# A new order of transfers and works in the opening of a RetNet and gelu kernel

The kernel computes a recurrent attention block and a feed-forward block behind it. The change touches the first 30 microseconds or so: which transfers go first, how TensorE is kept busy before its first data arrive, which of two operands is transposed first, and where the conversion of the weights stands among VectorE's other works.

## The chip, the cores and the metric

The kernel runs on one core of a Trainium2 chip. Its engines are TensorE (PE; PEld is its loading of weights), VectorE (DVE), ScalarE (ACT), GpSimd (POOL) and SyncE (SP), which here only issues transfers. The metric is the device time of one execution in microseconds (us); the figure quoted is the median of three.

## The reference

```python
# q, k, v: (4, 8, 768, 64); w_in: (512, 2048); w_out: (2048, 512); all float32
gamma = 1.0 - 2.0 ** (-5.0 - np.arange(H))
for t in range(S):
    state = gamma * state + outer(k[:, :, t], v[:, :, t])     # a 64x64 state for each batch and head
    y[:, :, t] = scale * q[:, :, t] @ state
x = y.transpose(0, 2, 1, 3).reshape(B * S, H * D)             # (3072, 512)
h = x @ w_in                                                  # (3072, 2048)
g = h * (1.0 / (1.0 + np.exp(-1.702 * h)))
return g @ w_out                                              # (3072, 512)
```

The launch hands `w_in` and `w_out` to the kernel as 64-bit words (float64), so the kernel converts them to float32 itself with integer operations.

## The kernel before

The recurrence is done in chunks of 64 time steps, two batches at a time: "pair j" below is chunk j of a pair of batches. For each pair, `q`, `k` and `v` are loaded (two transfers of 128 KB each), q and k are transposed on TensorE against an identity matrix (`turn`), copied out by ScalarE (`turned`), multiplied with each other (`step`, first part), masked by VectorE (`masked`), and multiplied with v and with the running state (`step`, second part). `step1` without a second number is the first part for pair 1; `step-0` is the second part for pair 0.

```python
def turn(j):
    ...
        x = QKV.pop(("q", j)), QKV["kn", j]
        TURNED[j] = p = [ps.tile([P, HP, P], F32, name="pt", tag="y") for i in range(2)]
        for n in (1, 0) if j else (0, 1):             # pair 0: q, then k; all others: k, then q
            for s in range(HP):
                for r in range(2):
                    pe.matmul(p[n][HALF[r], s, :], x[n][:, HP * r + s, :], ident, start=True, stop=True)   # L232
...
def turned(j):
    p = TURNED.pop(j)
    for n in (1, 0) if j else (0, 1):
        pin(act.activation((QT[j], KT[j])[n], p[n], AF.Copy))                                              # L243

def decay(j):                                          # k times its decay, by ScalarE; frees k's buffer
    ...
        for h in range(H):
            pin(act.activation(KD[j][:, h], x[:, h], AF.Copy, scale=d[:, h]))                              # L254

def attend(j, f=None):                                 # "stepj-f"
    pa = ps_a.tile([P, 2, 2, HP, D], F32, name="pa", tag="pa")       # one buffer: the next step waits for its readers
    if j is not None:
        ... pe.matmul(pa[..., 0, s, :], KT[j]..., QT[j]...)          # L265
    if f is not None:
        ... pe.matmul(pa[..., 1, s, :], kd..., vn...)                # L275, the new state
        ... pe.matmul(py[...], old..., qt...)                        # L284, by the state
        ... pe.matmul(py[...], vn..., a...)                          # L290, by the chunk itself
```

`masked` (L296), `state` (L301), `x` (L312 on VectorE; pair 0 by ScalarE, L314) and `updated` (L330 and L332) are VectorE's readers of these products; `x` writes the rows that the first feed-forward product needs. `state` makes the share of the running state, `updated` adds to the running state, and `aged` (ScalarE) decays it.

The weights of `w_in` come in blocks of 512 KB, `w0a`, `w0b`, `w1a` and so on. Each is converted in three works: `abs` on ScalarE, `half` and `rest` on VectorE:

```python
def start(self):                                       # "abs"
    pin(act.activation(self.m, self.hi.bitcast(F32), AF.Abs, scale=2.0 ** 16))                             # L189
def half(self):
    pin(dve.tensor_scalar(m, m, ..., op0=ALU.min, op1=ALU.max))                                            # L193
    pin(dve.tensor_scalar(mu, mu, 3, None, op0=ALU.logical_shift_left))                                    # L194
    pin(dve.scalar_tensor_tensor(hi, hi, 0x80000000, mu, ...))                                             # L195
def rest(self):
    pin(dve.tensor_scalar(mu, hi, 0xFF800000, None, op0=ALU.bitwise_and))                                  # L199
    pin(dve.scalar_tensor_tensor(lo.bitcast(F32), lo, 2.0 ** -52, m, ...))                                 # L200
    pin(dve.tensor_add(self.w, b, a))                                                                      # L204
```

Pair 0's weights are converted as two blocks of their own (`abs0a`, `half0b` and so on); later blocks go two at a time (`abs2`). The opening and the list of works, in whose order each engine and the transfer queue run (one order per engine), read before:

```python
def begin():
    for i in range(2):
        pin(pool.dma_start(cold[HALF[i]]..., ...))     # columns of decays
    pin(pool.dma_start(row, row_decay[None, :, 0:D]))  # the row of decays
    make_identity(nc, ident)
    dve.memset(ones, 1.0)
    dve.memset(first, 0.0)

def keep_warm():
    pe.matmul(idle..., ident, ident[:, None, :].to_broadcast([P, 4, P]), start=True, stop=True)            # L554

begin()
for name in """
    k0 table q0 warm turn0 w0b rows warm k1 abs0b q1 turned0 step0 v0 w0a half0b mask turn1 causal
    rest0b masked0 decay0 v1 decay1 abs0a half0a step-0 updated0 turned1 q2 step1 rowd k2 whole w2b
    turn2 w2a x0 k3 aged1 masked1 turned2 v2 rest0a abs2 q3 step-1 updated1 state1 decay2 aged2 step2 q4
    x1 half2 decay3 w3b w3a up0.0.0 masked2 turn3 k4 step-2 v3 q5 rest2 k5 gate0.0.0 turned3 updated2
    gated0.0.0 state2 step3 up0.0.2 masked3 ...
""".split():
    works[name]()
```

`k0` is issued from ScalarE's queue; all other loads of q, k, v and the weights in this list from SyncE's. `rows` spreads the row of decays over the partitions with a product (L560), `mask` and `causal` make the mask of it, and `up0.0.0` (L384) is the first product of the feed-forward block. `warm` is a product whose result nobody reads; its purpose is TensorE's clock.

Of the kernel before, what the change touches and what calls it, by code (L numbers as in the profile page):

```python
# [13 lines left out]
P = 128  # L14
# [14 lines left out]
def kernel(  # L29
# [29 lines left out]
    pe, act, dve, pool, sp = nc.tensor, nc.scalar, nc.vector, nc.gpsimd, nc.sync  # L59
    ctx.enter_context(tc.manual_schedule(engines={mybir.EngineType.PE}))  # L60

    B, H, S, D = q.shape
# [28 lines left out]
    X = const.tile([P, 7, 2, TH], F32, name="X")  # L91
# [4 lines left out]
    rowd = const.tile([P, HP, D], F32, name="rowd")  # L96
    row = G[0:1, 4, 0:2].rearrange("p a (h t) -> p (a h) t", t=D)
    ones = G[0:1, 4, 2, 0:P]
    cold = const.tile([P, 2 * H], F32, name="cold")
    whole = const.tile([P, HP], F32, name="whole")  # L100
    ident = const.tile([P, P], F32, name="ident")
    mask = const.tile([P, 2, HP, D], F32, name="mask")
# [5 lines left out]
    def pin(i):  # L108
        return tc.keep_in_program_order(i) if ordered[0] else i
# [4 lines left out]
    def load(j, what="qkv"):  # L114

        b, c = j // NC * 2, j % NC
        rows = slice(c * D, (c + 1) * D)
        keep = tc.keep_in_program_order if j < 2 * CB else lambda i: i  # L120

        def plain(name, src, tag, bufs, engine=sp):
            t = two.tile([P, H, D], F32, name=name + "_in", tag=tag, bufs=bufs)
            QKV[name, j] = t
            for i in range(2):
                keep(engine.dma_start(t[i * D:(i + 1) * D], src[b + i, :, rows, :].rearrange("h p d -> p h d")))  # L126

        if j < 2 * CB:
            if "q" in what:
                plain("q", q, "q_sq", 2)  # L130
            if "k" in what:
                plain("kn", k, "k_sq", 2, sp if j else act)
        elif "q" in what:
            for name, src in (("q", q), ("k", k)):
                t = two.tile([P, HP, P // C4, C4], F32, name=name + "_sq")
                for r0 in range(0, P, C4):
                    d0, h0 = r0 % D, r0 // D * HP
                    for n in range(P // C4):
                        t0 = c * D + n * C4 % D
                        tc.keep_in_program_order(sp.dma_start(  # L140
                            t[r0:r0 + C4, :, n], src[b + n * C4 // D, h0:h0 + HP, t0:t0 + C4, d0:d0 + C4]
                            .rearrange("h p d -> p h d")))
                QKV[name, j] = t
        if "v" in what:
            if j >= 2 * CB and c < NC - 1:
                plain("kn", k, "kn", 1)
            plain("v", v, "v", 2)
# [65 lines left out]
    def home(j, name):  # L213

        at = ["qT", "kT", "kd", "at"].index(name)
        shape = [[HP, P], [HP, P], [H, D], [2, HP, D]][at]
        if j >= 2 * CB:
            return one.tile([P] + shape, F32, name=name, tag=name, bufs=[2, 1, 1, 2][at])
        t = G[:, at, j % 2 * 2:j % 2 * 2 + 2].rearrange("p s t -> p (s t)")
        return t.rearrange("p (a b c) -> p a b c", a=2, b=HP) if at == 3 else t.rearrange("p (a b) -> p a b", a=shape[0])  # L220

    def turn(j):

        QT[j], KT[j] = home(j, "qT"), home(j, "kT")
        if j < 2 * CB:

            x = QKV.pop(("q", j)), QKV["kn", j]
            TURNED[j] = p = [ps.tile([P, HP, P], F32, name="pt", tag="y") for i in range(2)]
            for n in (1, 0) if j else (0, 1):
                for s in range(HP):  # L230
                    for r in range(2):
                        pe.matmul(p[n][HALF[r], s, :], x[n][:, HP * r + s, :], ident, start=True, stop=True)  # L232
        else:
            for t, name in ((QT[j], "q"), (KT[j], "k")):
                tc.keep_in_program_order(dve.transpose(
                    t.rearrange("p h t -> p (h t)"), QKV.pop((name, j)).rearrange("p h s d -> p (h s d)")))
        if 2 * CB <= j < NCH - 2:
            load(j + 2, "qk")

    def turned(j):  # L240
        p = TURNED.pop(j)
        for n in (1, 0) if j else (0, 1):
            pin(act.activation((QT[j], KT[j])[n], p[n], AF.Copy))  # L243

    def decay(j):
# [290 lines left out]
    m3 = mask.rearrange("p r h t -> p (r h) t")  # L536
    first = const.tile([P, 1], F32, name="first")
    idle = ps.tile([P, 4 * P], F32, name="idle", tag="x")
    works, products = {}, {}

    def begin():
        for i in range(2):

            pin(pool.dma_start(
                cold[HALF[i]].rearrange("p (n h) -> p n h", n=2),
                bass.AP(tensor=col_decay.tensor, offset=col_decay.offset, ap=[[W, D], [D * W + H, 2], [1, H]])))
        pin(pool.dma_start(row, row_decay[None, :, 0:D]))
        make_identity(nc, ident)
        dve.memset(ones, 1.0)
        dve.memset(first, 0.0)  # L550

    def keep_warm():

        pe.matmul(idle.rearrange("p (a b) -> p a b", a=4), ident, ident[:, None, :].to_broadcast([P, 4, P]),  # L554
                  start=True, stop=True)

    def rows():

# [32 lines left out]
    for j in range(2 * CB):  # L591
        for name in "qkv":
            works[f"{name}{j}"] = lambda j=j, name=name: load(j, name)
        works |= {f"{name}{j}": lambda j=j, do=do: do(j) for name, do in (
            ("turn", turn), ("turned", turned), ("decay", decay), ("masked", masked), ("state", by_state),
            ("x", output), ("aged", aged), ("updated", updated))}
        for f in (None, *range(2 * CB)):
            works[f"step{j}" + ("" if f is None else f"-{f}")] = lambda j=j, f=f: attend(j, f)
        works[f"step-{j}"] = lambda j=j: attend(None, j)
    for i in range(2 * NFF):  # L600
        works[f"w{i // 2}{'ab'[i % 2]}"] = lambda i=i: fetch(i)
    for name, i in [("0a", 0), ("0b", 1)] + [(str(p), 2 * p) for p in range(1, NFF)]:
        n = Narrow(i)
# [21 lines left out]


    begin()
    for name in """
        k0 table q0 warm turn0 w0b rows warm k1 abs0b q1 turned0 step0 v0 w0a half0b mask turn1 causal
        rest0b masked0 decay0 v1 decay1 abs0a half0a step-0 updated0 turned1 q2 step1 rowd k2 whole w2b  # L630
        turn2 w2a x0 k3 aged1 masked1 turned2 v2 rest0a abs2 q3 step-1 updated1 state1 decay2 aged2 step2 q4
        x1 half2 decay3 w3b w3a up0.0.0 masked2 turn3 k4 step-2 v3 q5 rest2 k5 gate0.0.0 turned3 updated2
        gated0.0.0 state2 step3 up0.0.2 masked3 abs3 half3 x2 rest3 turn4 w1b step-3 aged3 gate0.0.2 turned4
        state3 w1a w5b updated3 v5 decay4 k6 abs1 x3 gated0.0.2 q6 turn5 half1 up0.0.3 turned5 up0.1.2 step4
        aged4 w5a rest1 v4 gate0.0.3 decay5 w6a masked4 turn6 gate0.1.2 abs5 w6b step5-4 gated0.0.3 half5
        rest5 up0.0.1 updated4 turned6 k7 abs6 gated0.1.2 state4 gate0.0.1 w4b up0.1.1 half6 aged5
        gated0.0.1 w8a up0.0.5 rest6 masked5 decay6 w4a q7 up0.1.5 gate0.1.1 x4 gate0.0.5 gated0.1.1
        gated0.0.5 abs4 step6-5 w8b half4 gate0.1.5 state5 updated5 turn7 turned7 aged6 abs8 w9b up0.1.6
        gate0.1.6 x5 v6 masked6 gated0.1.5 step7-6 v7 w9a decay7 up0.1.0 rest4 w7a masked7 abs9 updated6
        state6 x6 gated0.1.6 w7b half8 step-7 state7 up0.1.4 gate0.1.4 abs7 x7 up1.8 rest8 half7 up1.5  # L640
        gated0.1.4 gate1.8 gated1.8 w11a rest7 half9 up1.4 gate1.4 w10b gated1.4 w10a w11b up0.0.7 gate0.1.0
        up1.0 gated0.1.0 gate0.0.7 rest9 up1.3 gate1.0 gated1.0 abs10 gated0.0.7 w12a gate1.5 gate1.3 up1.2
        gated1.5 gated1.3 gate1.2 w12b up1.6 gated1.2 gate1.6 abs11 up1.9 gate1.9 half11 rest11 up1.11
        gated1.9 gated1.6 up0.0.4 up0.1.7 abs12 w14b half10 gate0.0.4 rest10 aged7 up0.0.6 gate1.11 updated7
        gated1.11 gated0.0.4 up1.10 gate0.1.7 w14a half12 gate0.0.6 gated0.1.7 abs14 half14 w13a gate1.10
        gated0.0.6 rest12 w13b up1.7 gate1.7 up1.12 up1.13 gated1.10 gate1.13 rest14 gated1.7 gated1.13
        abs13 half13 gate1.12 w15a up1.15 gate1.15 gated1.15 w15b late_loads up1.14 abs15 gated1.12 up0.1.3
        half15 rest13 up1.1 gate1.14 gated1.14 rest15 gate0.1.3 gate1.1 gated1.1 gated0.1.3
    """.split():
        works[name]()  # L650
    ordered[0] = False
    def chunks(first, last):

        return [s for j in range(first, last + 1)
                for s in (lambda j=j: turn(j), lambda j=j: step(j, j - 1))]
# [72 lines left out]
```

## Time and profile before

| what | before |
| --- | --- |
| median of three executions | 685.57 us (683.95 to 686.31) |
| span of the profiled execution | 683.3 us |
| TensorE busy, loading of its weights busy | 668.9 us, 558.7 us |
| VectorE, ScalarE, GpSimd busy | 367.1 us, 151.1 us, 125.5 us |
| moved by transfers | 46.55 MB, of which most packets are under 512 B |

The page cuts the span into 40 slices of about 17 us and gives each engine's busy share as a digit in tenths. These are its rows for TensorE and the transfers:

```profile
PE   6899999999999999999999999999999999999997
...
DMA  7887631332222224301333310313310210000001
```

TensorE is below nine tenths in the first two slices and the last one only; the transfers are densest in the first four. "Busy" for TensorE is modelled at the ends of pipelined products, and the granted clock of the page is what the throttle granted; whether products run at half speed is read from their own durations.

### The profile page before, as it was taken

To read this page: it belongs to the slowest core of one execution; us is meant where nothing else is said; L and a number is where in the kernel's file an instruction comes from. 1 tells how busy PE (TensorE), PEld (TensorE's weight loads), DVE (VectorE), ACT (ScalarE), POOL (GpSimd) and SP (SyncE) were. 2 spreads that over 40 slices of the span, in tenths; PEclk is the share of its full clock that TensorE was granted. 3 is DMA by queue.
4 is the path that set the end of the run, shared out by engine and by line. 5 is a ranking of instruction groups with operands and counts; after the bars stand their busy time and mean duration, and the time that the engine had idled before them with its cause. 6 is when DMAs were issued, how large, how long until landed. Compare 5 with 4: busy or idle time off the path is not lost.

```text
span 683.3 us, 13882 instructions
## 1 busy us (share of the span) xinstructions
PE 668.9 (98%) x5830; PEld 558.7 (82%) x5830; DVE 367.1 (54%) x514; ACT 151.1 (22%) x293; POOL 125.5 (18%) x116
## 2 busy tenths in 40 slices
PE   6899999999999999999999999999999999999997
PEld 4788854757788888888888888888888888888886
DVE  3899994989811843443752453563345372345241
ACT  5775423221000001332000332000333000233000
POOL 3000000000467414000434000244100243000030
PEclk9999999999999999999999999999999999999999
DMA  7887631332222224301333310313310210000001
GB/s 179 231 236 212 177 130 62 123 84 35 49 34 64 61 45 103 58 1 16 73 57 84 54 32 9 75 31 89 72 40 3 50 45 32 16 0 1 16 0 47
DMA packets 140334, 46.55 MB, mean 68 GB/s; under 512 B 131824, under 2 KB 132848, under 8 KB 140272
## 3 DMA queue, kind: packets, MB, share of 16 engines
q1 hardware_dynamic: 136352, 39.10, 24.9%
q0 software_dynamic: 1760, 5.26, 2.0%
q10 hardware_dynamic: 2160, 1.31, 0.6%
q8 instruction: 46, 0.75, 0.5%
q14 instruction: 16, 0.13, 0.1%
HBM read 39.33 MB, written 6.29 MB: 67 GB/s over the span
## 4 chain that ended last, share of the span: by engine, by line
PE 84%; DVE 7%; SPq 5%; DMA 1%; issue 1%; ACT 1%; ACTq 0%
PE pd L503 37%; PE px L435 16%; PE py L435 12%; PE ph L384 6%; SPq L140 4%; PE ph L396 4%; PE pa L265 2%; PE pt L232 2%; PE py L290 2%; PE pa L275 2%; PE py L284 2%; SPq L126 1%; PE pd L488 1%; DVE G L425 1%; DMA W<-in_moe_w_out_dram 1%
## 5 line engine op out<-in xcount | busy, mean ns | idle before, releaser
L503 PE MATMUL pd<-W,G 128*128 128x256 f32 x1088 | 240.5, 381 | 1.3 <-issue 0.9
L503 PEld LDWEIGHTS pd<-W,G 128*128 128x128 f32 x1088 | 205.2, 190 | 30.4 <-DVE G L426 1.2
L435 PE MATMUL px<-X,W 128*128 128x256 f32 x512 | 119.0, 379 | 0.0
L435 PEld LDWEIGHTS px<-X,W 128*128 128x128 f32 x512 | 97.3, 190 | 13.2
L435 PE MATMUL py<-X,W 128*128 128x256 f32 x384 | 90.7, 379 | 0.0
L435 PEld LDWEIGHTS py<-X,W 128*128 128x128 f32 x384 | 73.0, 190 | 9.9
L384 PE MATMUL ph<-X,W 128*128 128x256 f32 x256 | 57.6, 382 | 0.0
L396 PE MATMUL ph<-W,W 128*128 128x512 f32 x128 | 55.6, 592 | 0.0
L384 PEld LDWEIGHTS ph<-X,W 128*128 128x128 f32 x256 | 48.1, 190 | 8.2 <-issue 1.0
L256 POOL TENSOR_TENSOR kd<-kn_in,cold 128x512 f32<-128x512 f32 x14 | 16.4, 1173 | 187.5 <-PE pa L275 163.8
L396 PEld LDWEIGHTS ph<-W,W 128*128 128x128 f32 x128 | 24.3, 190 | 28.9 <-issue 28.4
L427 POOL TENSOR_TENSOR G<-G 128x512 f32<-128x512 f32 x20 | 29.5, 1480 | 91.8 <-DVE G L426 91.8
L356 ACT ACTIVATE sg<-G 128x512 f32<-128x512 f32 x48 | 30.3, 630 | 51.3 <-DVE G L445 31.0
L361 DVE TENSOR_TENSOR G<-G,sg 128x512 f32<-128x512 f32 x48 | 33.5, 699 | 13.7 <-ACT sg L356 13.7
L296 DVE TENSOR_TENSOR at<-pa,mask 128x512 f32<-128x512 f32 x16 | 11.0, 686 | 54.7 <-PE pa L275 54.7
L324 POOL TENSOR_TENSOR state<-state,whole 128x512 f32<-128x512 f32 x13 | 13.5, 1038 | 128.1 <-DVE state L332 127.9
L503 PE MATMUL pd<-W,W 128*128 128x256 f32 x160 | 35.8, 381 | 1.0 <-DVE W L426 1.0
L503 PEld LDWEIGHTS pd<-W,W 128*128 128x128 f32 x160 | 30.2, 190 | 6.3 <-DVE W L426 1.8
L475 ACT ACTIVATE u<-pd 128x512 f32<-128x512 f32 x6 | 3.6, 597 | 137.3 <-PE pd L503 137.3
L356 ACT ACTIVATE sg<-ph 128x512 f32<-128x512 f32 x32 | 18.9, 595 | 66.2 <-PE ph L396 32.9
L480 POOL DMA_DIRECT2D out_dram<-o x20 | 14.9, 745 | 91.4 <-DVE o L479 91.4
L445 DVE TENSOR_TENSOR G<-py,p 128x512 f32<-128x512 f32 x16 | 11.1, 692 | 38.1 <-PE py L435 38.1
(112 smaller groups left out, 676.0 us busy)
## 6 DMA issues: line engine op xcount, KB each, us to landing
W<-in_moe_w_in_dram SPq DMA_DIRECT2D x12, 512.0 KB, 6.1
v_in<-in_v_dram SPq DMA_DIRECT2D x48, 128.0 KB, 3.3
kn_in<-in_k_dram SPq DMA_DIRECT2D x42, 128.0 KB, 3.4
W<-in_moe_w_out_dram SPq DMA_DIRECT2D x10, 512.0 KB, 4.4
out_dram<-o POOLq DMA_DIRECT2D x20, 256.0 KB, 2.7
q_sq<-in_q_dram SPq DMA_DIRECT2D x256, 16.0 KB, 1.9
k_sq<-in_k_dram SPq DMA_DIRECT2D x256, 16.0 KB, 1.9
G<-in_moe_w_out_dram SPq DMA_DIRECT2D x6, 512.0 KB, 3.9
```

Source lines behind the costliest of these rows:

```text
L140: tc.keep_in_program_order(sp.dma_start(t[r0:r0 + C4, :, n], src[b + n * C4 // D, h0:h0 + HP, t0:t0 + C4, d0:d0 + C4] .rearrange("h p d -> ...
L232: pe.matmul(p[n][HALF[r], s, :], x[n][:, HP * r + s, :], ident, start=True, stop=True)
L256: pool.tensor_mul(KD[j], x, d.to_broadcast([P, H, D]))
L265: pe.matmul(pa[HALF[i], r, 0, s, :], KT[j][HALF[r], s, HALF[i]], QT[j][HALF[r], s, HALF[i]], start=True, stop=True)
L356: pin(act.activation(s, h, AF.Sigmoid, scale=1.702))
L361: pin(dve.tensor_mul(g, h[:, i], s[:, i]))
L384: pe.matmul(h[:, ab], w, X[:, 2 * th + c // 2, c % 2, :], start=(ab == 0 and c == 0), stop=(c == 3), skip_group_check=True)
L396: pe.matmul(h, w, X1[:, c // 2:4:2, c % 2, :], start=(c == 0), stop=(c == 3))
L427: pool.tensor_sub(a[1], a[1], a[0])
L435: pe.matmul(acc[:, u, :], W1[:, 2 * d + u, sa, c, :], X[:, sb, c, :], start=(start and u == 0 and c == 0), stop=(stop and c == 1), skip_gr ...
L480: (pool if m < NB - 1 else act).dma_start(rows[th, e], o)
L503: pe.matmul(p0[:, n, :], g1(m, p, sa)[:, n * P:(n + 1) * P], W2[:, sb, p, :], start=(new and p == 0 and n == 0), stop=(last and p == NP - ...
```

## The change

Five things are done at once.

- The transfer queue: `w0b` goes ahead of q0 and `w0a` ahead of k1; `w2b` and `w2a` now go ahead of k2, where they followed it. The aim is to give VectorE blocks to convert early.
- Warming: VectorE clears a block of zeros (a part of X that is written much later), and four products of it run before `rows` and `turn0`. Before, one product of the identity ran ahead of `turn0` and one behind `rows`. The zeros need not wait for GpSimd's identity.
- The row of decays is loaded ahead of the columns, and `rows` stands ahead of `turn0`.
- Pair 0's k is turned ahead of its q, as with every other pair.
- VectorE's works between `masked0` and `updated2` stand in another order: `half0a` ahead of `masked0`, `rest0a` ahead of `updated0`, `half2` behind `updated1`. On TensorE, `up0.0.0` stands ahead of `step2`.

```diff
-            for n in (1, 0) if j else (0, 1):
+            for n in (1, 0):
...
-        for n in (1, 0) if j else (0, 1):
+        for n in (1, 0):
...
+    blank = X[:, 0].rearrange("p a t -> p (a t)")
...
     def begin():
+        pin(dve.memset(blank, 0.0))
+        pin(pool.dma_start(row, row_decay[None, :, 0:D]))
         for i in range(2):
             pin(pool.dma_start(cold[HALF[i]]..., ...))
-        pin(pool.dma_start(row, row_decay[None, :, 0:D]))
         make_identity(nc, ident)
...
     def keep_warm():
-        pe.matmul(idle.rearrange("p (a b) -> p a b", a=4), ident, ident[:, None, :].to_broadcast([P, 4, P]),
-                  start=True, stop=True)
+        pe.matmul(idle, blank[:, 0:P], blank, start=True, stop=True)
...
-        k0 table q0 warm turn0 w0b rows warm k1 abs0b q1 turned0 step0 v0 w0a half0b mask turn1 causal
-        rest0b masked0 decay0 v1 decay1 abs0a half0a step-0 updated0 turned1 q2 step1 rowd k2 whole w2b
-        turn2 w2a x0 k3 aged1 masked1 turned2 v2 rest0a abs2 q3 step-1 updated1 state1 decay2 aged2 step2 q4
-        x1 half2 decay3 w3b w3a up0.0.0 masked2 turn3 k4 step-2 v3 q5 rest2 k5 gate0.0.0 turned3 updated2
+        k0 w0b table q0 warm warm warm warm rows turn0 w0a abs0b half0b k1 q1 turned0 step0 mask causal v0 rest0b
+        abs0a turn1 half0a masked0 decay0 v1 turned1 rest0a step-0 w2b updated0 q2 rowd decay1 x0 step1 masked1 w2a
+        whole k2 turn2 aged1 step-1 state1 x1 k3 turned2 v2 updated1 abs2 q3 decay2 aged2 up0.0.0 step2 q4
+        half2 decay3 w3b w3a masked2 turn3 k4 step-2 v3 q5 rest2 k5 gate0.0.0 turned3 updated2
         gated0.0.0 state2 step3 up0.0.2 masked3 ...
```

## The prediction

> **What bounds the kernel now.** I read the page's busy times first, then a table of stretches, then the order of time of the opening, and last the transfers. The page's first part gives each engine's busy time, share of the span and instruction count:
>
> ```profile
> PE 668.9 (98%) x5830; PEld 558.7 (82%) x5830; DVE 367.1 (54%) x514; ACT 151.1 (22%) x293; POOL 125.5 (18%) x116
> ```
>
> TensorE is the bound. The table of stretches (columns: stretch, its length, then busy time and instructions of each engine, granted clock, DMA share, GB/s) says where it is not:
>
> ```profile
> 0.00:10.00 10.00, 4.71 (x28) 3.17 (x30) 0.17 (x2) 2.05 (x3) 2.60 (x9) 1.00 0.68 159
> 10.00:20.00 10.00, 8.21 (x188) 5.96 (x187) 8.15 (x14) 9.11 (x29) 2.83 (x4) 1.00 0.89 231
> 20.00:30.00 10.00, 8.61 (x189) 7.43 (x186) 9.35 (x13) 8.00 (x26) 0.00 (x0) 1.00 0.87 227
> 30.00:40.00 10.00, 9.96 (x286) 8.73 (x282) 8.56 (x12) 6.00 (x14) 0.00 (x0) 1.00 0.81 205
> 40.00:100.00 60.00, 60.00 (x801) 48.02 (x794) 56.87 (x78) 27.75 (x66) 0.00 (x0) 1.00 0.67 191
> ```
>
> TensorE idles 5.3 + 1.8 + 1.4 = 8.5 us in the first 30 us and hardly at all in the 70 us after. The order of works beyond turn3 is the same before and after, so what the change is worth is the shift of TensorE's work at about 30 us, and no more than a few us of 685. In TensorE's order of time (start, length, line, what; in brackets the idle time before it and what ended it):
>
> ```profile
> 7.37 1.98 PE L232 MATMUL pt<-ident,q_in 128*64 128x128 f32 x16 [1.42 <-DMA q_in<-in_q_dram]
> 9.10 1.87 PE L232 MATMUL pt<-ident,kn_in 128*64 128x128 f32 x16
> ...
> 13.00 0.69 PE L265 MATMUL pa<-G 64*64 64x64 f32 x32
> ...
> 18.48 0.69 PE L265 MATMUL pa<-G 64*64 64x64 f32 x32 [1.41 <-DVE state L330]
> 19.24 1.09 PE L232 MATMUL pt<-ident,kn_in 128*64 128x128 f32 x16
> 20.13 1.07 PE L232 MATMUL pt<-ident,q_in 128*64 128x128 f32 x16
> ...
> 24.72 0.45 PE L265 MATMUL pa<-G 64*64 64x64 f32 x12 [1.35 <-issue]
> 25.10 3.72 PE L384 MATMUL ph<-X,W 128*128 128x256 f32 x16
> ```
>
> These are turn0 (7.37), step0 (13.00), step1 (18.48), turn2 (19.24), the end of step2 (24.72) and the first hidden product, up0.0.0 (25.10). turn3 follows at 28.75 and step3 at 32.31. turn2 starts 0.14 us after the second half of k2 lands: the trace has its landing at 19.10.
>
> The transfers, all on one queue in program order (start, time to issue, what):
>
> ```profile
> 11.69 1.27 SPq L126 DMA_DIRECT2D q_in<-in_q_dram  x2
> 13.53 2.34 SPq L126 DMA_DIRECT2D kn_in<-in_k_dram  x2
> 15.91 1.66 SPq L163 DMA_DIRECT2D G<-in_moe_w_in_dram  x2
> ```
>
> The reader is to see that k2 (13.53) goes ahead of the two blocks of w2 (15.91), and that landing comes some 5 us after issue. The third line carries w2b and w2a (their raw buffer is a part of G), whose landings the trace has at 20.13 and 22.72.
>
> [...] turn0's halves take 1.98 and 1.87 us, the same work at 19.24 takes 1.09, and between lie the 3.6 us of turn0. Its gap from 17.1 to 18.5 us did not bring the half clock back. [...] q, k and v come in 256-byte packets, at 220 to 240 KB/us in the best microseconds and 150 to 180 in most; weights come in 2048-byte packets at 320 to 360. [...] k0 from ScalarE's queue will share with w0b as it shares with q0 now (landings 6.28 and 7.23).
>
> **The change part by part.**
>
> Warming. It removes two products of the identity (the first waits for GpSimd's identity at 3.88) and puts in four of zeros. They wait for a memset of 128x512; I estimate 0.4 us from VectorE's 0.43 for a tensor_scalar of that shape, so it ends at about 1.3. A warm product is two instructions, 1.13 us now when warm and 2.08 when cold with the drain. Back to back I take 1.7 cold and 0.85 warm, so two cold and two warm give 1.4 + 3.4 + 1.7 = 6.5. rows (0.85) needs the row of decays, which lands at 7.95 now and is issued 1.3 us earlier, about 6.6. So TensorE is free at 7.4.
>
> turn0. With w0b between, I put k0 at 7.0 and q0 at 8.0. k turns 7.4 to 8.3, q to 9.3 (0.95 a half at full clock), ScalarE's copy of q (0.60) to 9.9. step0 can start at 10.0 against 13.00: 3.0 us earlier.
>
> Conversion. w0b leads the queue and lands at about 6.5 instead of 9.42. VectorE's three half0b operations (0.43 + 0.43 + 0.69) then end at 8.8, the mask (0.69) and GpSimd's triangle (1.85) at 11.3, rest0b at about 11. abs0a on ScalarE takes 10.0 to 10.7, half0a on VectorE 1.6 more to 12.3, masked0 0.7 to 13.0, step-0 (1.2) to 14.2. rest0a (1.9) now lies before updated0 (0.7), which ends at 15.6. step1, which reuses the accumulator that updated0 reads, starts at 15.6 against 18.48: 2.9 us earlier.
>
> turn2. Here the gain meets the new order of transfers. w0b, q0, w0a, k1, q1, v0, v1, w2b, q2, w2a, k2: both blocks of w2 now stand ahead of k2, 1.0 MB more. Two ways to T, the landing of k2:
> - Bytes: eight loads of 256 KB at 1.15 us and four blocks at 1.5 us are 15.2 us; with the first packet at 2.4 and 1 to 2 us from last packet to landing, 18.6 to 19.6 if the engines never starve. By the same sum the kernel before would have k2 at about 16.1 and has it at 19.10, so up to 3 us are lost to starving. Blocks between the small loads should lose less.
> - Issue: k2 needs k0's buffer, free when decay0 (2.0 us on ScalarE after abs0a) ends at 12.7. In the trace eight landing semaphores go round, so at most eight transfers are under way. I put the issue at 13.7 to 14.3; with 5 to 6.6 us to landing, as transfers behind weight blocks have now, 19.3 to 20.9.
> I choose T = 19.7. turn2 stands before step-1 in TensorE's fixed order, so TensorE idles from 16.3 to 19.7.
>
> After turn2. turn2 is 1.9, step-1 1.6, then VectorE makes state1 and x1 (2 x 0.69 and 0.1), which up0.0.0 needs: it starts at T + 5.1. up0.0.0 3.65, step2 0.65: TensorE reaches turn3 at T + 9.4, which is 29.1 against 28.75. VectorE lags more. After x1 it has updated1 and half2 (0.7 + 2.65) and must wait for step2, since up0.0.0 now precedes it: masked2 ends at T + 10.2, rest2 (3.2) at T + 13.4, updated2 (0.7) at T + 14.1, and step3 needs the accumulator that updated2 reads. step3 at T + 14.1 = 33.8 against 32.31: 1.5 us later. From there the order is the old one and TensorE the bound, so the sum is 685.57 + 1.5 = 687.1; I say 687.0.
>
> **The rivals.**
> 1. The opening's gain of 2.9 us is kept. That needs k2 by 16.5. For it: weight packets are fast and fill the queue. Against it: 15.2 us of packets cannot land by then. A part of it is possible (T of 18 and rest2 off the path): the time would be 683.5 to 685.
> 2. The half clock comes back. [...] Against it, the present gap of 1.4 us is harmless. It would cost about 1.5 us more: 688.5.
> 3. The gap of 1.35 us inside step2 ("issue") stays. I left it out because TensorE will have been idle before. Nothing in the profile names its cause; if it comes back, 1.3 us more.
> 4. Nothing moves: VectorE is busy 56.87 of 60 us from 40 to 100 us, so a start earlier or later could be taken up there. Against it, TensorE has no idle time there to give. 685.6.
>
> **Range and chances.** The sum stands or falls with T: a us in T is a us of time. T from 18 to 21 gives 685.4 to 688.4; rivals 1 to 3 and the 1 us or so by which the runs before differ (683.95 to 686.31) widen this to 683.8 to 689.4. Two per cent are 13.7 us, more than all the idle time of the opening, so both outer chances are about nothing.
>
> **What would show it.** Right, step by step: the first hidden warm product near 1.4; turn0 with k first at 7 to 8 and each half near 1.0 us; step0 near 10; step1 near 15.6; then an idle time of about 3 us before turn2 that ends with DMA of k; turn2 near 19.7; step3 near 33.8. Wrong: turn2 right behind step1, or step3 at 32.3 or earlier (then the time falls), or turn2's halves at 1.9 us each (the half clock). If step3 comes late and the time is still 685 or less, a later stage held slack that I did not see.

## The result and the profile after

The changed kernel takes 688.77 us (median, 688.18 to 689.22) against 685.45 for the kernel before on the same chip: a ratio of 1.005, 95% interval 1.0031 to 1.007. It is slower by about 3.3 us (2.1 to 4.8 by the interval). The profiled execution spans 686.4 us instead of 683.3.

Busy times of the changed kernel's page, first part (busy time, share, instructions):

```profile
PE 671.6 (98%) x5834; PEld 560.0 (82%) x5834; DVE 367.5 (54%) x515; ACT 151.2 (22%) x293; POOL 125.7 (18%) x116
```

No engine has more work to speak of; only TensorE's busy time grew, by 2.7 us. The table of stretches of the changed kernel, with the columns of before:

```profile
0.00:10.00 10.00, 8.47 (x30) 3.86 (x32) 3.19 (x8) 2.15 (x3) 2.91 (x10) 1.00 0.91 209
10.00:20.00 10.00, 5.29 (x176) 4.52 (x172) 7.18 (x12) 9.05 (x28) 2.56 (x4) 1.00 0.91 225
20.00:30.00 10.00, 7.46 (x139) 6.92 (x140) 3.83 (x6) 5.98 (x18) 0.00 (x0) 0.83 0.68 180
30.00:40.00 10.00, 8.83 (x211) 7.67 (x210) 8.58 (x12) 5.48 (x14) 0.00 (x0) 1.00 0.67 159
```

The first ten us look better, filled with warming products, and VectorE begins early (3.19 instead of 0.17). Then TensorE is busy 5.29 instead of 8.21, VectorE only 3.83 us from 20 to 30 where it had 9.35, and from 20 to 30 us the granted clock (the third figure from the end) is 0.83. TensorE in order of time:

```profile
8.87 1.09 PE L232 MATMUL pt<-ident,kn_in 128*64 128x128 f32 x16
9.80 1.04 PE L232 MATMUL pt<-ident,q_in 128*64 128x128 f32 x16
11.54 0.69 PE L265 MATMUL pa<-G 64*64 64x64 f32 x32 [0.70 <-ACT G L243]
...
16.84 0.69 PE L265 MATMUL pa<-G 64*64 64x64 f32 x32 [1.27 <-DVE state L330]
20.93 1.97 PE L232 MATMUL pt<-ident,kn_in 128*64 128x128 f32 x16 [3.39 <-DMA kn_in<-in_k_dram]
22.66 1.71 PE L232 MATMUL pt<-ident,q_in 128*64 128x128 f32 x16
...
27.54 3.72 PE L384 MATMUL ph<-X,W 128*128 128x256 f32 x16 [1.61 <-DVE X L312]
31.19 0.69 PE L265 MATMUL pa<-G 64*64 64x64 f32 x32
31.82 1.09 PE L232 MATMUL pt<-ident,kn_in 128*64 128x128 f32 x16
...
36.52 0.69 PE L265 MATMUL pa<-G 64*64 64x64 f32 x32 [1.17 <-DVE state L332]
```

In this pair of traces the changed kernel leads by 1.64 us down to step1 (16.84 against 18.48); the experiments below show that this lead is not the change's. Then turn2 waits 3.39 us for k2 and runs at half speed: its halves take 1.97 and 1.71 us. step3 (36.52) is 4.2 us behind the 32.31 of before. The transfer queue shows why k2 is late:

```profile
11.04 0.62 SPq L163 DMA_DIRECT2D G<-in_moe_w_in_dram  x1
11.78 1.27 SPq L126 DMA_DIRECT2D q_in<-in_q_dram  x2
13.10 0.62 SPq L163 DMA_DIRECT2D G<-in_moe_w_in_dram  x1
13.99 4.93 SPq L126 DMA_DIRECT2D kn_in<-in_k_dram  x4
```

k2 is issued at nearly the same time as before (13.99; it was 13.53), but with both blocks of w2 ahead of it (11.04 and 13.10). The trace has its two landings at 20.58 and 20.79 instead of 18.48 and 19.10. The half clock is seen best in single microseconds of the changed kernel:

```profile
20.00:21.00 1.00, 0.07 (x2) 0.10 (x4) 0.00 (x0) 0.00 (x0) 0.00 (x0) 0.79 0.79 180
21.00:22.00 1.00, 1.00 (x10) 1.00 (x12) 0.00 (x0) 0.00 (x0) 0.00 (x0) 0.50 0.86 195
...
24.00:25.00 1.00, 1.00 (x52) 0.83 (x51) 0.00 (x0) 0.53 (x2) 0.00 (x0) 1.00 0.00 0
```

The clock is granted by half from 20.58 to 24.00 us, 3.41 us long, from the trace's clock record. Of the 4.2 us at step3, 3.1 remain in the span. One wait accounts for 0.9 of the difference; where the rest went was not traced. Among TensorE's waits beyond 60 us (waiter, what ended it, us in total, times, longest) the kernel before has this one, at 339 us, which ends with nothing that the profile shows; the changed kernel has none such:

```profile
PE pd L503 <- issue: 0.9, 1, 0.9
```

### The profile page after: what moved, and what is told of

Read it like the earlier page. It is cut to its first block, busy times and chain, and to the rows that moved or that the text cites. A ratio compares the mean times of both kernels' runs of the same rounds, so it can differ in the third digit from the quotient of the medians.

```text
span 686.4 us, 13893 instructions
## 1 busy us (share of the span) xinstructions
PE 671.6 (98%) x5834; PEld 560.0 (82%) x5834; DVE 367.5 (54%) x515; ACT 151.2 (22%) x293; POOL 125.7 (18%) x116
## 4 chain that ended last, share of the span: by engine, by line
PE 91%; DVE 4%; DMA 3%; SPq 1%; ACT 1%; issue 0%; ACTq 0%; DVEq 0%
PE pd L503 38%; PE px L435 16%; PE py L435 12%; PE ph L384 8%; PE ph L396 8%; PE pa L265 2%; DMA kn_in<-in_k_dram 2%; PE pt L232 2%; PE py L290 2%; PE py L284 1%; PE pa L275 1%; SPq L140 1%; PE pd L488 1%; DVE G L425 1%; DMA v_in<-in_v_dram 1%; DVE G L426 1%
```

## The experiments

The theory: k2 behind both blocks of w2 costs the whole, by the late landing and by the half clock behind the idle time (turn2's halves of 1.97 and 1.71 us behind 3.39 us of waiting). The main rival: the new order of works behind turn2 (up0.0.0 ahead of step2, state1 and x1 ahead of updated1; half2 follows updated1 in both kernels). Each experiment was timed against the kernel before on one chip; the profile's own milestones are in the table. All times are us.

| kernel | step1 | k2 landed | turn2 | step3 | median | ratio to before, 95% interval |
| --- | --- | --- | --- | --- | --- | --- |
| before | 18.48 | 19.10 | 19.24 | 32.31 | 685.45 | |
| changed | 16.84 | 20.79 | 20.93 | 36.52 | 688.77 | 1.0031 to 1.007 |
| k2 ahead of both blocks | 16.15 | 18.13 | 18.27 | 32.37 | 684.18 | 0.9985 to 1.0007 |
| k2 between the blocks | 15.92 | 19.25 | 19.39 | 34.82 | 686.82 | 1.0018 to 1.0046 |
| before, with w2 ahead of k2 | 16.72 | 21.53 | 21.67 | 35.41 | 688.62 | 1.0041 to 1.0071 |
| three warming products in the gap | 16.04 | 21.72 | 21.86 | 37.57 | 688.46 | 1.0036 to 1.0072 |
| five warming products in the gap | 16.43 | 20.23 | 21.54 | 35.65 | 687.93 | 1.0038 to 1.0086 |
| old order behind turn2 | 16.66 | 21.17 | 21.30 | 36.25 | 687.38 | 1.0027 to 1.0056 |
| k2 ahead and old order | 16.79 | 17.83 | 17.97 | 30.80 | 683.49 | 0.9981 to 1.0009 |
| the same, decay0 early | 16.85 | 17.36 | 17.50 | 30.34 | 682.48 | 0.996 to 0.998 |
| w0a later too | 14.63 | 16.48 | 16.62 | 29.75 | 682.86 | 0.9961 to 0.9991 |

Beside the runs below the second row the kernel before had medians of 684.33 to 684.48, a us less than beside the changed kernel; so rows of different origin are compared by their ratios. Milestones are of one execution each and wander: the opening of before has its step1 at 18.48 and at 16.72 us in its two traces (rows 1 and 5), and in the four kernels with the same transfers up to k2 (rows 2, 6, 7 and 8) k2 landed between 20.23 and 21.72 us.

**k2 ahead of both blocks.**

```diff
-  rest0a step-0 w2b updated0 q2 rowd decay1 x0 step1 masked1 w2a
-  whole k2 turn2 aged1 ...
+  rest0a step-0 updated0 q2 rowd decay1 x0 step1 masked1
+  whole k2 w2b w2a turn2 aged1 ...
```

> The changed kernel with k2 loaded ahead of w2b and w2a, all else as changed. If the place of k2 in the queue is the cause: k2 lands near 18 us instead of 20.8, turn2 starts near 18.2 with halves of 1.0 to 1.1 us (full clock), step3 near 32.3 (turn2 + 14.1) instead of 36.5, and the time falls by about 4 us to 684 to 685. If VectorE's and TensorE's order behind turn2 is the cause: turn2 early but step3 still near 36, and the time stays at 688 to 689.

TensorE of this kernel:

```profile
16.15 0.70 PE L265 MATMUL pa<-G 64*64 64x64 f32 x32 [1.27 <-DVE state L330]
18.27 1.09 PE L232 MATMUL pt<-ident,kn_in 128*64 128x128 f32 x16 [1.42 <-DMA kn_in<-in_k_dram]
...
23.40 3.72 PE L384 MATMUL ph<-X,W 128*128 128x256 f32 x16 [1.61 <-DVE X L312]
...
32.37 0.69 PE L265 MATMUL pa<-G 64*64 64x64 f32 x32 [1.17 <-DVE state L332]
```

Its transfer queue:

```profile
13.31 1.27 SPq L126 DMA_DIRECT2D kn_in<-in_k_dram  x2
14.62 1.14 SPq L163 DMA_DIRECT2D G<-in_moe_w_in_dram  x2
```

k2 is issued 0.7 us earlier than in the changed kernel and lands 2.7 us earlier: its two halves take 4.3 and 4.2 us from issue to landing instead of 6.6 and 6.2. turn2 comes 2.7 us earlier at full clock, step3 4.15 us earlier, and the time is that of the kernel before. This one move takes the whole loss away. The two waits behind turn2, 1.61 for x1 and 1.17 for updated2, are the same as in the changed kernel: they belong to the new order of works, and were not what made it slower than before.

**The kernel before with w2 ahead of k2.** The same move the other way round, with nothing else of the change.

```diff
-  updated0 turned1 q2 step1 rowd k2 whole w2b
-  turn2 w2a x0 k3 ...
+  updated0 turned1 w2b q2 step1 rowd w2a k2 whole
+  turn2 x0 k3 ...
```

> The kernel before with one part of the change alone: w2b and w2a loaded ahead of k2. If the place of k2 is the cause: k2 lands near 21 us, turn2 starts near 21 instead of 19.24 and, [...] at half clock; time 687 to 689. If the cause is the order of works: turn2 waits a little and VectorE's old order takes it up; time 685 to 686.

TensorE of this kernel:

```profile
16.72 0.69 PE L265 MATMUL pa<-G 64*64 64x64 f32 x32 [1.30 <-DVE state L330]
21.67 1.97 PE L232 MATMUL pt<-ident,kn_in 128*64 128x128 f32 x16 [4.25 <-DMA kn_in<-in_k_dram]
23.40 1.69 PE L232 MATMUL pt<-ident,q_in 128*64 128x128 f32 x16
```

The wait for k2 and the half clock are there again, with a ratio (1.0056) beside that of the whole change (1.005). VectorE's old order took up little of it: turn2 is 2.4 us later than in the kernel before and the half clock costs 1.5 more (measured below), and step3 (35.41) is 3.1 us later.

The opening of this kernel, down to step1, is that of before, and yet its step1 is at 16.72, where the trace of before has 18.48: q0 had landed at 5.18 us instead of 7.23. So the changed kernel's 16.84 shows no gain of its opening.

**k2 between the blocks.** Half of the cost: w2b ahead of k2, w2a behind it.

```diff
-  step1 masked1 w2a
-  whole k2 turn2
+  step1 masked1
+  whole k2 w2a turn2
```

> The changed kernel with only w2a moved behind k2; w2b stays ahead of it: half of the suspected cost. If each block of 512 KB ahead of k2 costs its time on the queue: k2 lands near 19.4, half way between 18.1 (both behind) and 20.8 (both ahead), turn2 near 19.5 mostly at full clock, time near 686. If the landing depends on the issue alone: 18 or 21 and a time of 684 or 688.8.

k2 landed at 19.25, about half way (18.13, 19.25, 20.79), and the time lies between as well (ratios 0.9996, 1.0032, 1.005). The two blocks of 512 KB cost k2 1.1 and 1.5 us of landing in these three traces, and the kernel 0.36% and 0.18%, that is 2.5 and 1.2 us; the landing wanders by 1.5 us with the same transfers ahead of it, and the interval of this kernel overlaps that of the change, so how the loss divides between the two blocks is not shown. The profiled execution was not at full clock throughout, against what I expected (mean granted clock 0.997): behind a gap of 2.77 us turn2's halves took 1.97 and 1.55 us.

```profile
19.39 1.97 PE L232 MATMUL pt<-ident,kn_in 128*64 128x128 f32 x16 [2.77 <-DMA kn_in<-in_k_dram]
21.12 1.55 PE L232 MATMUL pt<-ident,q_in 128*64 128x128 f32 x16
```

The 20 executions of this kernel sort by their mean granted clock: eight at 1.000 have a median of 684.6, eight at 0.997 or 0.998 have 687.0, four at 0.995 have 688.6. One half-clock stretch of 3.41 us, the length in the changed kernel's trace, takes 0.25% from the mean clock of a span, so by this estimate these are none, one and two of them. The sorting is not clean proof of the clock's cost, since a later k2 makes the gap longer as well, and in the traces the half clock stands behind the longer gaps (2.77 us and more, not 1.42).

**Three warming products in the gap.** A trial of the half clock alone.

```diff
+  def keep_warm_i(): pe.matmul(idle..., ident, ident[:, None, :].to_broadcast([P, 4, P]), ...)
-  decay1 x0 step1 masked1 w2a
+  decay1 x0 step1 warmi warmi warmi masked1 w2a
```

> The changed kernel with three more warming products (of the identity) behind step1, in TensorE's idle time before turn2. If the half clock costs what it seems: turn2's halves take 1.0 to 1.1 us instead of 1.97 and 1.71, step3 comes 1.4 us earlier (35.1), and the time falls by 1.4 us to about 687.3. If the half clock is hidden behind another wait (x1, updated2): no change, 688.8.

It decided nothing in the profile: the products ended at 19.51, k2 landed late in that execution (21.72), TensorE idled 2.35 us again, and the mean granted clock of the execution was 0.998. The ratio is that of the change. Its nine executions sort by clock as well: five at 0.999 or 1.000 have a median of 687.1 us, four at 0.997 or 0.998 have 689.7. The same reservation holds.

**Five warming products in the gap.** The same with five.

> The changed kernel with five warming products in the gap before turn2 instead of three: they take TensorE to about 21[...]. If the half clock costs 1.5 to 2 us: the clock stays full in nearly all executions, turn2 at 21 to 22 with halves of 1.0 to 1.1 us, time 686.8 to 687.3. If it costs nothing: 688.5.

TensorE of this kernel:

```profile
17.05 4.56 PE L560 MATMUL idle<-ident 128*128 128x512 f32 x10
21.54 1.09 PE L232 MATMUL pt<-ident,kn_in 128*64 128x128 f32 x16
22.46 1.04 PE L232 MATMUL pt<-ident,q_in 128*64 128x128 f32 x16
...
30.95 1.09 PE L232 MATMUL pt<-ident,kn_in 128*64 128x128 f32 x16
```

Now the clock stays full (mean 1.000, turn2's halves 1.09 and 1.04 us): turn2 to turn3 takes 9.41 us (21.54 to 30.95) instead of 10.89 (20.93 to 31.82). The half clock's cost at this place is thus 1.5 us. The products themselves hold turn2 back (k2 had landed at 20.23), which gives part of it back: step3 comes 0.9 us earlier than in the changed kernel. In the time nothing of it is seen (1.0062 against 1.005, the intervals overlap widely, and this kernel was timed four times only): how the loss of time divides between the late k2 and the half clock is not shown. As a remedy it is poor; as a measurement of the local cost it is clear.

**The old order behind turn2.** Transfers and opening as changed, the order of works of before from turn2 to turn3.

```diff
-  turn2 aged1 step-1 state1 x1 k3 turned2 v2 updated1 abs2 q3 decay2 aged2 up0.0.0 step2 q4
-  half2 decay3 w3b w3a masked2 turn3
+  turn2 aged1 k3 turned2 v2 abs2 q3 step-1 updated1 state1 decay2 aged2 step2 q4 x1
+  half2 decay3 w3b w3a up0.0.0 masked2 turn3
```

> The changed kernel with the works behind turn2 in the order of before (updated1 first, step2 and half2 ahead of up0.0.0); transfers and opening as changed. If the new order behind turn2 costs what the sum of the prediction says: turn2 still near 20.9 at half clock, but step3 at about 34.7 instead of 36.5, and the time falls by 1.8 us to about 687.0. If k2 alone is the cause: step3 and the time stay, 688.8.

TensorE of this kernel:

```profile
21.30 1.98 PE L232 MATMUL pt<-ident,kn_in 128*64 128x128 f32 x16 [3.95 <-DMA kn_in<-in_k_dram]
23.04 1.95 PE L232 MATMUL pt<-ident,q_in 128*64 128x128 f32 x16
...
36.25 0.69 PE L265 MATMUL pa<-G 64*64 64x64 f32 x32
```

step3 no longer waits for updated2, but this execution was at half clock for longer (mean 0.995; the products of L275 behind turn2 took 1.13 us, 0.69 in the changed kernel), so its milestones cannot be set beside the changed kernel's. The ratio of 1.0041 is 0.6 us below that of the change, and the intervals overlap: neither the 1.8 us expected nor their absence is shown by this run alone. In TensorE's milestones they can be seen elsewhere: the kernel before with w2 ahead of k2 has the old order and half speed in turn2 alone (halves 1.97 and 1.69 us, then 0.69 for L275), and its step3 is at turn2 + 13.74; the changed kernel's is at turn2 + 15.59 (the two differ in their openings too).

**k2 ahead and the old order.** Only the change's opening is left.

> The changed kernel with k2 ahead of both blocks of w2 and with the order of before behind turn2: what is left of the change is its opening alone. If the new order behind turn2 costs about 1.1 us of its own (step3 at turn2 + 13 instead of + 14.1): turn2 near 18.3, step3 near 31.3 instead of 32.4, time 683.0 to 683.5 where k2 ahead alone gave 684.2. If that order costs nothing once k2 is early: 684.2 again.

step3 is at turn2 + 12.8, where k2 ahead with the new order had turn2 + 14.1: 1.3 us in the profile. The medians are 683.49 and 684.18, but the ratios (0.9995 and 0.9996) do not differ, so a cost of the new order is seen in TensorE's waits and not settled in the time. What the opening (zeros, k first, w0b first) brings by itself is not separated from nothing (0.9981 to 1.0009).

**The same with decay0 early.** decay0 moves on ScalarE ahead of turned0, to free k0's buffer.

```diff
-  k1 q1 turned0 step0 ...
-  abs0a turn1 half0a masked0 decay0 v1 turned1 ...
+  k1 q1 decay0 turned0 step0 ...
+  abs0a turn1 half0a masked0 v1 turned1 ...
```

> The same, and decay0 on ScalarE ahead of turned0, so that k0's buffer comes free some 3 us earlier. If k2's wait for k0's buffer now sets turn2: k2 is issued near 12.3 instead of 13.3 and lands near 16 to 17, turn2 follows step1 (near 17), step3 comes near 30, time about 682. If the transfers ahead of it set its landing: k2 lands near 18 as before and the time is that of the run without it.

TensorE of this kernel:

```profile
16.85 0.69 PE L265 MATMUL pa<-G 64*64 64x64 f32 x32 [1.32 <-ACT G L254]
17.50 1.09 PE L232 MATMUL pt<-ident,kn_in 128*64 128x128 f32 x16
```

turn2 follows step1 without a wait, step3 is at 30.34, and the kernel is faster than the kernel before (ratio 0.996 to 0.998) and than the run without decay0's move (682.48 against 683.49 us on the same chip). The way there was only half as expected: k2 was issued at 13.34, not 12.3. decay0 had long ended (10.5), but the queue was still issuing v1 (from 10.53) and q2 (from 11.96), about 0.65 us for each transfer of 128 KB. Why the time falls is not shown: step3 comes only 0.46 us earlier than in the run without, and the execution traced here (683.54 us) was slower than the one traced there (682.96).

**w0a later too.** w0a behind v0, updated0 ahead of abs0a and half0a, rest0a just ahead of turn2, decay0 in its old place.

```diff
+  k0 w0b table q0 warm warm warm warm rows turn0 abs0b half0b k1 q1 turned0 step0 mask causal v0 w0a rest0b
+  turn1 masked0 decay0 v1 turned1 step-0 updated0 abs0a half0a q2 rowd decay1 x0 step1 masked1
+  whole k2 w2b w2a rest0a turn2 ... (old order)
```

> The changed kernel with all its small loads up to v0 ahead of w0a, v1, q2 and k2 ahead of w2, decay0 in its old place, updated0 ahead of half0a, and the order of before behind turn2. If what stands ahead of k2 in the queue and of updated0 on VectorE sets the opening: k2 lands near 16.5, step1 near 15.7, turn2 near 16.6, step3 near 29.6, time about 681.8, a little below the run with decay0 early (682.5). If another wait takes over behind turn2 (rest0a or the conversion of w2, now late on VectorE, ahead of up0.0.0): turn2 early, step3 at 30.5 or later and a time of 682.5 to 683.5.

The milestones came as expected (step1 14.63, turn2 16.62, step3 29.75), but the time is 682.86, no better than with decay0 early (ratios 0.9976 and 0.997). The 0.6 us by which step3 leads is still there at the end of the two traces (spans of 680.7 and 681.3 us), but the traced execution with decay0 early was 1.1 us above its median, so it is no measure of the two kernels. Three of the 13 executions here had a granted clock of 0.997 (median 684.4), none of the 21 with decay0 early.

## Why the prediction was right, and where its terms were too small

**The mechanism held step by step.** Whatever the opening gained was lost in a wait of TensorE for k2; the wait predicted as 16.3 to 19.7 (3.4 us) was 17.54 to 20.93 (3.39). That its length came out to the hundredth is luck: both of its ends were 1.2 us late. TensorE then waited for x1 and for updated2, as worked out. step3 at T + 14.1 came out as 14.1 after turn2 in both runs of the new order at full clock (18.27 to 32.37, 21.54 to 35.65).

**T was too early by 1.1 us.** 19.7 was chosen, 20.79 measured. The issue was as estimated (13.99 and 14.63, for 13.7 to 14.3), and 6.2 to 6.6 us from issue to landing is the upper end of the 5 to 6.6 taken from the trace. (In the three other kernels with the same transfers ahead of it, k2 landed at 20.23, 21.17 and 21.72.) I leant to the lower sum, that of bytes, which assumes that the engines hardly starve; transfers behind weight blocks had shown the longer time already (up to 6.4 us for a load of k in the kernel before).

**The half clock should have been in the sum.** It was rival 2, at 1.5 us, and stood outside. That an idle time of 3.4 us could bring it back was an assumption of mine: no trace of the kernel before shows it. The traces behind the change do: in the changed kernel the clock was halved for 3.41 us behind a gap of 3.39 us (the 3.41 us ahead of the fall held 0.37 us of products), and with k2 between the blocks a gap of 2.77 us was enough. The cost of 1.5 us was right (9.41 and 10.89 us from turn2 to turn3). What spoke against it, that the gap of 1.4 us ahead of step1 in the kernel before is harmless, was read from one trace: of the 107 executions of that kernel beside the experiments 30 had a mean granted clock of 0.995 to 0.998, by my estimate a stretch of 3.41 us at half clock or two; where in the kernel is not known. The two terms, 1.1 for T and 1.5 for the clock, with 33.8 for step3 make 36.4; measured 36.52.

**Smaller misses.** step1 came at 16.84, not 15.6, and all of that lies ahead of turn0, which began at 8.87 where I had 7.4: step1 follows turn0 by 7.96 to 7.99 us in all seven traces with this opening, for 8.2 in the sum. Six of the eight warming instructions ran cold (1.06 to 1.22 us each; the other two 0.66 and 0.59) where I took four, and they and `rows` held turn0 back, since k0 had landed at 7.34. It did not matter, since T set turn2. Rival 3, the gap inside step2, did not return in the new order; it shows again in kernels with the old order once k2 is early (1.20 us with k2 ahead and the old order). That its end lies 0.03 to 0.5 us behind the end of x1 in every profile that has it suggests a wait for x1; this was not tested. And a start 4.2 us later was 3.1 at the end, 0.9 of it by the wait at 339 us that only the kernel before has of the two; the time is 3.3 above before, for 1.5 predicted.

## What to carry to other kernels

When a block is moved forward in a queue to feed one engine, look up what the pacing engine waits for next, and whether that load is now behind the block: here k2 landed at 18.13 us ahead of both blocks of w2 and at 20.79 behind them. An idle time of TensorE can cost more than itself: here the products behind gaps of 2.77 to 4.25 us ran at half speed (the first half of turn2 took 1.97 or 1.98 us), which cost TensorE 1.5 us in the changed kernel, and behind gaps of 0.49 to 1.42 us it took 1.09. Count the half clock into the sum as soon as the estimated gap comes near those that had it. Here both were cured by letting the load that TensorE needs first go first (with k2 ahead of both blocks 16 of 20 executions had a granted clock of 0.999 or 1.000, in the changed kernel none of four), not by more warming.

## What the runs showed of the hardware

In the changed kernel's trace the clock is at half from 20.58 to 24.00 us, for 3.41 us; it came back while turn2 was running. In the traced executions that waited for k2 ahead of turn2 and had no warming products there, the gap and the speed of turn2 were these:

| kernel | idle ahead of turn2, us | turn2's halves, us | mean granted clock |
| --- | --- | --- | --- |
| k2 ahead and old order | 0.49 | 1.09, 1.07 | 1.000 |
| w0a later too | 1.29 | 1.09, 1.07 | 1.000 |
| k2 ahead of both blocks | 1.42 | 1.09, 1.07 | 1.000 |
| k2 between the blocks | 2.77 | 1.97, 1.55 | 0.997 |
| changed | 3.39 | 1.97, 1.71 | 0.997 |
| old order behind turn2 | 3.95 | 1.98, 1.95 | 0.995 |
| before, with w2 ahead of k2 | 4.25 | 1.97, 1.69 | 0.998 |

These are single executions, and others of the same kernels differ: with k2 between the blocks 8 of 20 had a mean granted clock of 1.000, with w2 ahead of k2 in the kernel before 2 of 9. What the difference hangs on was not shown.

Products of zeros lift the clock as others do. In the changed kernel they ran from 1.53 us, six of them at 1.06 to 1.22 us, and the trace's clock record begins, at full, at 6.93; the two behind took 0.66 and 0.59 us. In the kernel before, with two products of the identity from 3.88 us (1.22 and 1.06 us) and turn0 from 7.37 (halves 1.98 and 1.87), it begins at 10.75; the next two products of the identity, from 11.95, took 0.70 and 0.59 us.
